# Attention and a gated feed-forward layer with seven-product block matmuls: work shifted by a slot, products reordered, odd tiles paired

## The chip, the core and the metric

The kernel runs on one core of one Trainium2 chip. Five engines work side by side there: TensorE (PE, matmuls; its weight loads are listed as PEld), VectorE (DVE), ScalarE (ACT), GpSimd (POOL, which here issues the loads) and SyncE (SP, which here issues transposes and stores). The metric is the device time of one execution in microseconds (us); lower is better. A profile is one execution recorded instruction by instruction, and its span runs from the first instruction to the last.

## What is computed

```python
# q, k, v: 8 batches, 12 heads, 448 tokens, 64 dims, float32
scores = q @ k.T / sqrt(64) - log(448)
attn   = 1 / (1 + exp(-scores))              # a sigmoid, no row sums
x      = (attn @ v), heads side by side      # 3584 tokens x 768
gate   = max(x @ w_gate, 0)                  # 768 x 1536
val    = x @ w_val                           # 768 x 1536
out    = (gate * val) @ w_out                # 1536 x 768, float32
```

## The kernel before, in words

The matmuls take 16-bit operands and add up in PSUM, which has 8 banks; a ring named `free` hands them out, and `later` (line 84) puts the ones just taken into an order for their next use. The order of all instructions on each engine is the order in which the code below emits them.

**Attention.** A batch is 3 groups of 4 heads. Queries and keys are transposed in 7 chunks of 64 tokens, on PE for batches 0 and 1 and for later ones by DMA: `dma_transposes` (211) makes two DVE copies into `rel` and has SP issue one transposing DMA. `qk_unit` (292) makes the scores of one chunk in two banks, and ACT takes the sigmoid of each into a tile PT. A batch has 21 such units. `pv_group` (300) multiplies a group's 7 tiles with v, and DVE copies the two results to `xT` (184), the transposed input of the feed-forward layer.

**Feed-forward.** Batches 0 and 1 (token group 0) make gate and val by plain matmuls: `gv` (304), one unit for each of 12 blocks of 128 columns. ACT takes the relu and DVE multiplies into `hT` (327). The other token groups, of two batches each, treat gate and val as one 2 x 2 block product, in seven block products instead of eight (a Strassen-Winograd scheme): `gv_pair` (498) does two column blocks at once, 42 matmuls of 448 columns. It needs sums of weight blocks (`unit_sums`, and once for all `gate_sums`, 469) and of input blocks (`batch_sums_t1` and `batch_sums`, 488 and 492), all on DVE. The down projection, `hT` times `wo`, is done for a pair of token tiles of 128 in the same way: `down_pair` (423), 42 matmuls of 384 columns in seven products of six. It needs `weight_sums` (395) once, and four sums for each pair (`token_sums`, 406). With the blocks of a pair's tokens A11, A12, A21, A22 the sums are S1 = A21 + A22, S2 = S1 - A11, S4 = A12 - S2, and S3 = A11 - A21, which overwrites A21 in `hT`. The products are called P1 = A11 B11, P2 = A12 B21, P3 = S4 B22, P4 = A22 T4, P5 = S1 T1, P6 = S2 T2 and P7 = S3 T3. Before the change they are issued in the order P1 P5 P6 P2 P7 P3 P4. Three banks hold them: b takes P1, P6, P7 and P4, c takes P5 and P3, and a takes P2. Between the products ACT and DVE move partial sums to SBUF, and the next product into b or c waits for the copy before it.

A token group has 896 tokens: 7 tiles, three pairs and tile 6, which goes alone through `down` (341): 24 plain matmuls.

**Slots.** The loop from line 684 cuts each batch's 21 units into 5 or 6 slots m. A slot emits 3 to 5 units, perhaps a `pv_group` among them, and then its feed-forward work: a few `gv` (`ffn_mix`, with hooks placed after a count of them), or, from batch 2's last slot on, one item of the queue `work` (`next_work`, 667). An item is "w" (a `gv_pair`), "t" (the single tile) or "y" (a `down_pair`). Small jobs of the slot (transposes for the next batch, batch sums, loads) are emitted inside the item: in a pair behind the copy of P1, by the call `beside()`. `prepare` (659) makes the sums that the next item needs; a pair calls it as `then()` before P4. A group's items are pushed in slot 0 of the following even batch, and what is left after batch 7 runs alone:

```python
    def push_group(g):
        tail = [("t", g, 6)] + [("y", g, p) for p in range(3)]
        if g == 0:
            tail.insert(0, tail.pop(1))
        work.extend([("w", g, f) for f in range(0, NFC, 2) if g > 0] + tail)
```

`hold` (637) is a tiny POOL copy that waits for a transposed tile, so that loads issued behind it start later; `late_loads` (644) places one before v of batch 2 and `wo` (`load_o`, 162). In batch 1 to 3 the loads of the next batch's k, q and v stand behind these on POOL.

Of the kernel before, what the change touches and what calls it, by code (L numbers as in the profile page):

```python
# [17 lines left out]
def kernel(  # L18
# [143 lines left out]
    def load_o():  # L162
        for m0, m1 in ((0, 512), (512, DM)):
            nc.gpsimd.dma_start(
                wo[:, :, m0:m1], moe_w_out[:, m0:m1].rearrange("(c p) m -> p c m", p=P)
            )
# [96 lines left out]
    class FirstSlot:  # L263
# [6 lines left out]
        def unit(self, u):  # L270
# [8 lines left out]
            i = (self.number * 4 + u) % 12  # L279
            PT = early.tile([P, 2, 512], FP16, tag=f"PT{i}", name="PT")  # L280
# [22 lines left out]

    def gv(b, q0, qn, f, act_relu):
# [19 lines left out]
        if g not in hT_tiles:  # L324
            hT_tiles[g] = hTp.tile([P, NFC, 2 * S], FP16, tag="hT", name="hT")
        o = (b % 2) * S + q0
        nc.vector.tensor_tensor(  # L327
            out=hT_tiles[g][:, f, o : o + qn],
            in0=gate_sb[:, 0:qn],
            in1=ps[1][:, 0:qn],  # L330
            op=AOP.mult,
        )
# [8 lines left out]
    def down(g, t):  # L341
        ysb = ysbp.tile([P, DM], FP32, tag="ysb", name="ysb")
        for nm, m0, m1 in (("ya", 0, 512), ("yb", 512, DM)):
            ps = bank(nm)
            for f in range(NFC):
                nc.tensor.matmul(  # L346
                    ps[:, 0 : m1 - m0],
                    hT_tiles[g][:, f, t * P : (t + 1) * P],
                    wo[:, f, m0:m1],
                    start=(f == 0),  # L350
                    stop=(f == NFC - 1),
                )
            nc.vector.tensor_scalar(
                out=ysb[:, m0:m1], in0=ps[:, 0 : m1 - m0], scalar1=OUT_SCALE, scalar2=None, op0=AOP.mult
            )
        store(g, t, ysb, 0, DM, (nc.sync, nc.sync))

# [7 lines left out]
    late = {}  # L365
    sums = {}

    def open_late():
        first_sbuf.close()
        pool = ctx.enter_context(tc.tile_pool(name="late", bufs=1))  # L370
        late["T"] = pool.tile([P, 4, HF, HM], FP16, tag="T", name="T")
        late["X"] = pool.tile([P, 3, HD, S], FP16, tag="X", name="X")
        late["sums"] = ctx.enter_context(tc.tile_pool(name="sums", bufs=2))
# [20 lines left out]

    def weight_sums(i):
        T = [late["T"][:, j] for j in range(4)]
        B11, B21 = wo[:, 0:HF, 0:HM], wo[:, HF:NFC, 0:HM]
        B12, B22 = wo[:, 0:HF, HM:DM], wo[:, HF:NFC, HM:DM]
        sub(T[i], *((B12, B11), (B22, T[0]), (B22, B12), (B21, T[1]))[i])

    def token_blocks(g, p):
        h = hT_tiles[g]
        t1, t2 = (slice(t * P, (t + 1) * P) for t in (2 * p, 2 * p + 1))
        return h[:, 0:HF, t1], h[:, HF:NFC, t1], h[:, 0:HF, t2], h[:, HF:NFC, t2]

    def token_sums(g, p):
# [3 lines left out]
        sub(S2, S1, A11)  # L410
        sub(S4, A12, S2)
        sub(A21, A11, A21)
        sums[("y", g, p)] = S1, S2, S4
# [9 lines left out]
    def down_pair(g, p, beside, then, last, first_copy):  # L423
        A11, A12, S3, A22 = token_blocks(g, p)
        S1, S2, S4 = sums.pop(("y", g, p))
        T1, T2, T3, T4 = (late["T"][:, i] for i in range(4))
        B11, B21, B22 = wo[:, 0:HF, 0:HM], wo[:, HF:NFC, 0:HM], wo[:, HF:NFC, HM:DM]
        y1, y2 = (ysbp.tile([P, DM], FP32, tag="ysb", name="ysb") for _ in range(2))
        lo, hi = slice(0, HM), slice(HM, DM)
        b, c, a = bank("u"), bank("y12"), bank("y11")  # L430
        later((7, 6, 5))
# [10 lines left out]
        first_copy(y1[:, lo], b)  # L442
        beside()
        product(c, S1, T1)
        scaled_act(y2[:, hi], c)
        product(b, S2, T2, False)
        scaled_act(y1[:, hi], b)
        product(a, A12, B21)
        plus(y1[:, lo], a)
        product(b, S3, T3, False)  # L450
        plus(y2[:, hi], b)
        product(c, S4, B22, False)
        plus(y1[:, hi], c)
        if last:
            store(g, 2 * p, y1, 0, DM, (nc.sync, nc.scalar))
        else:
            store(g, 2 * p, y1, 0, DM, (nc.sync, nc.sync))
# [3 lines left out]
        if last:  # L461
            store(g, 2 * p + 1, y2, HM, DM, (nc.sync, nc.sync))
            store(g, 2 * p + 1, y2, 0, HM, (nc.sync, nc.scalar))
        else:
            store(g, 2 * p + 1, y2, 0, DM, (nc.sync, nc.sync))
# [7 lines left out]
    def unit_sums(g, f):  # L473
        S1, S2, S4 = sums_tile(2 * P)
        fs = slice(f * P, (f + 2) * P)
# [5 lines left out]
        sums[("w", g, f)] = S1, S2, S4  # L481
# [10 lines left out]
    def batch_sums(g, ks):  # L492
        T1, T2, T4, _, B21, B12, B22 = batch_blocks(g, ks)
        sub(B12, B22, B12)
        sub(T2, B22, T1)
        sub(T4, B21, T2)

    def gv_pair(g, f, beside, first_copy):
# [3 lines left out]
        b, c, a = ([bank(nm) for _ in range(2)] for nm in ("u", "g2", "g1"))  # L502
        later((6, 7, 4, 5, 2, 3))
        gs = [[gsbp.tile([P, S], FP32, tag="gsb", name="gsb") for _ in range(3)] for _ in range(2)]
        if g not in hT_tiles:
            hT_tiles[g] = hTp.tile([P, NFC, 2 * S], FP16, tag="hT", name="hT")
        h = hT_tiles[g]
        sets = []
        for u in range(2):
            us, fs = slice(u * P, (u + 1) * P), slice((f + u) * P, (f + u + 1) * P)  # L510
            S1, S2, S4 = (t[:, :, us] for t in sums[("w", g, f)])
            sets.append((
                wg[:, 0:HD, fs], wg[:, HD:NDC, fs], wv[:, HD:NDC, fs],
                S1, S2, wv[:, 0:HD, fs], S4,
            ))
        del sums[("w", g, f)]

        def product(ps, i, W, first=True):
            for u in range(2):
                products([(ps[u], S, HD, sets[u][i], W, first)])  # L520

        def copy(i, ps, by=nc.scalar.copy):
            for u in range(2):
                by(gs[u][i][:], ps[u][:, 0:S])  # L524

        def plus(i, ps):
            for u in range(2):
# [4 lines left out]
        def gated(u, o, gate_sb, val):  # L532
            nc.vector.scalar_tensor_tensor(
                out=h[:, f + u, o : o + S], in0=gate_sb, scalar=0.0, in1=val, op0=AOP.max, op1=AOP.mult
            )

        product(b, 0, B11)
        copy(0, b, first_copy)
        product(c, 3, T1)
        copy(2, c)  # L540
        product(b, 4, T2, False)
        copy(1, b)
        beside()
        product(a, 1, B21)
        plus(0, a)
# [5 lines left out]
        for u in range(2):  # L551
            gated(u, 0, gs[u][0][:], b[u][:, 0:S])
        for u in range(2):
            gated(u, S, gs[u][1][:], gs[u][2][:])
# [89 lines left out]
    def late_loads():  # L644
# [3 lines left out]
        load_o()  # L648
# [3 lines left out]

    def push_group(g):
        tail = [("t", g, 6)] + [("y", g, p) for p in range(3)]
        if g == 0:
            tail.insert(0, tail.pop(1))
        work.extend([("w", g, f) for f in range(0, NFC, 2) if g > 0] + tail)
# [9 lines left out]
    def next_work(jobs=(), alone=False):  # L667
        kind, g, i = work.popleft()

        def beside():  # L670
            for job in jobs:
                job()

        if kind == "y":
            down_pair(g, i, beside, prepare, not work, scaled_act if alone else scaled)
        elif kind == "w":
            gv_pair(g, i, lambda: (prepare(), beside()), nc.scalar.copy if alone else nc.vector.tensor_copy)
        else:
            beside()
            prepare()  # L680
            down(g, i)

    ffn_mix(1, [(1, lambda: both(1, 0))])
    for b in range(1, B):
# [16 lines left out]
        elif b == 2:  # L701
            mix = (2, 2, 1, 1, 1, 2)
# [92 lines left out]
```

## Time and profile before

| | us |
|---|---|
| median of three runs (lowest, highest) | 401.42 (400.29, 402.0) |
| the profiled execution, its own time | 400.93 |
| span of that execution | 399.2 |
| pairs of group 0 start, PE | 93.48, 123.14, 132.26 |
| single tiles start, PE | 115.21, 200.07, 291.71, 369.30 |
| last matmul's start group, PE | 392.70 |

The profiled execution stands 0.5 us below the median, and the 1.7 us between its time and its span lie outside the recorded instructions. The mean granted TensorE clock was 0.999. An engine's busy share is a mean over the whole span; what a stage waits for is seen in the list of waits and in the timeline, where each row is a run of like instructions on one engine with its start, its duration, and in brackets the idle time before it with what ended that.

### The profile page before, as it was taken

How to read it: one execution, taken by the hardware profiler on the slowest of the kernel's cores; microseconds unless marked ns; L12 is line 12 of the kernel's file. 1: busy time of each engine (PE TensorE's matmuls, PEld its weight loads, DVE VectorE, ACT ScalarE, POOL GpSimd, SP SyncE). 2: the span in 40 equal slices, each digit the busy share in tenths (PEclk: the TensorE clock that was granted, in tenths of full speed). 3: DMA queues.
4: the chain of work that ended last, by engine and by line, in shares of the span. 5: the costliest groups of instructions: out<-in, count | busy, mean ns of one | idle time of the engine just before them, and what ended most of it. 6: DMA issues, size and time to landing. Idle time of an engine off the chain costs nothing.

```text
span 399.2 us, 8737 instructions
## 1 busy us (share of the span) xinstructions
PE 388.9 (97%) x3488; PEld 217.9 (55%) x3488; DVE 279.9 (70%) x539; ACT 223.0 (56%) x475; POOL 49.4 (12%) x73
## 2 busy tenths in 40 slices
PE   8999999999998999999999999999999999999994
PEld 3678786545455554554555555455455555555562
DVE  2454344367358889999758889999766779887661
ACT  5946778783885565655665455565566234533131
POOL 8643301600030300003000300000000000000000
PEclk9999999999999999999999999999999999999999
DMA  9999994999897894224945695223012320000144
GB/s 149 199 199 204 205 141 94 177 203 187 178 161 152 165 204 76 46 48 51 178 85 133 130 218 89 48 24 61 12 40 80 80 79 2 0 2 0 39 115 124
DMA packets 68793, 43.69 MB, mean 109 GB/s; under 512 B 35856, under 2 KB 65296, under 8 KB 68752
## 3 DMA queue, kind: packets, MB, share of 16 engines
q0 software_dynamic: 30736, 23.33, 39.1%
q1 hardware_dynamic: 37584, 19.24, 23.0%
q8 instruction: 27, 0.44, 0.5%
q10 hardware_dynamic: 432, 0.56, 0.4%
q14 instruction: 14, 0.11, 0.1%
HBM read 47.19 MB, written 11.01 MB: 146 GB/s over the span
## 4 chain that ended last, share of the span: by engine, by line
PE 73%; DMA 14%; issue 6%; POOL 3%; DVE 2%; ACT 1%; ACTq 0%; POOLq 0%; DVEq 0%
PE u L385 32%; PE g L385 15%; PE y L385 9%; DMA v<-in_v_dram 6%; PE qk_ps L232 5%; PE pv_ps L250 5%; DMA wo<-in_moe_w_out_dram 4%; DMA k<-in_k_dram 4%; PE ya L346 3%; PE v_ps L309 1%; PE yb L346 1%; PE g_ps L309 1%; POOL q L110 1%; POOL k L110 1%; DVE wv L376 1%
## 5 line engine op out<-in xcount | busy, mean ns | idle before, releaser
L187 ACT ACTIVATE PT<-qk_ps 128x448 f16<-128x448 f32 (+3 forms) x318 | 150.6, 594 | 71.2 <-PE qk_ps L232 71.1
L385 PEld LDWEIGHTS <-S 128*128 128x128 f16 x540 | 52.8, 98 | 44.4 <-issue 0.8
L528 DVE TENSOR_TENSOR gsb<-g,gsb 128x448 f32<-128x448 f32 x72 | 43.0, 625 | 14.5 <-PE g L385 13.8
L232 PE MATMUL qk_ps<-qkT 64*64 64x448 f16 (+2 forms) x756 | 50.0, 336 | 0.9 <-DVE qkT L206 0.5
L421 ACT ACTIVATE ysb<-u 128x384 f32<-128x384 f32 x27 | 13.4, 498 | 56.3 <-PE u L385 56.3
L327 DVE TENSOR_TENSOR hT<-gate_sb,v_ps 128x256 f16<-128x256 f32 (+2 forms) x36 | 16.2, 465 | 33.5 <-ACT gate_sb L318 22.4
L385 PEld LDWEIGHTS <-hT 128*128 128x128 f16 x288 | 27.7, 98 | 21.0 <-issue 3.2
L524 ACT COPY gsb<-u 128x448 f32<-128x448 f32 x48 | 25.8, 566 | 23.9 <-PE u L385 22.9
L250 PE MATMUL pv_ps<-PT,v 64*64 64x448 f16 (+2 forms) x756 | 37.4, 329 | 0.4 <-issue 0.4
L184 DVE TENSOR_SCALAR xT<-pv_ps 128x448 f16<-128x448 f32 (+2 forms) x53 | 27.9, 567 | 13.4 <-PE pv_ps L250 12.1
L232 PEld LDWEIGHTS <-qkT 64*64 64x64 f16 x756 | 20.3, 105 | 24.9 <-issue 16.3
L309 PE MATMUL v_ps<-xT,wv 128*128 128x256 f16 (+2 forms) x216 | 33.3, 291 | 0.4 <-DVE hT L327 0.2
L309 PE MATMUL g_ps<-xT,wg 128*128 128x256 f16 (+2 forms) x216 | 33.5, 292 | 0.1
L385 PEld LDWEIGHTS <-wv 128*128 128x128 f16 x216 | 21.1, 98 | 19.8
L385 PEld LDWEIGHTS <-wg 128*128 128x128 f16 x216 | 20.3, 98 | 20.6 <-issue 3.0
L250 PEld LDWEIGHTS <-v 64*64 64x64 f16 x756 | 21.8, 107 | 11.8 <-issue 1.4
L385 PE MATMUL u<-T,hT 128*128 128x384 f16 x144 | 27.3, 326 | 0.0
L437 DVE SCALAR_TENSOR_TENSOR ysb<-y,ysb 128x384 f32<-128x384 f32 x24 | 13.4, 557 | 18.8 <-PE y L385 11.3
L110 POOL DMA_DIRECT2D k<-in_k_dram x14 | 10.9, 779 | 112.3 <-DVE rel L215 105.8
L309 PEld LDWEIGHTS <-wg 128*128 128x128 f16 x216 | 18.5, 98 | 11.5 <-issue 5.0
L309 PEld LDWEIGHTS <-wv 128*128 128x128 f16 x216 | 20.1, 98 | 8.2 <-DMA wv<-in_moe_w_val_dram 0.5
L385 PE MATMUL u<-xT,wg 128*128 128x448 f16 x108 | 23.5, 353 | 0.1
(67 smaller groups left out, 531.3 us busy)
## 6 DMA issues: line engine op xcount, KB each, us to landing
out_dram<-ysb SPq DMA_DIRECT2D x53, 192.0 KB, 2.9
k<-in_k_dram POOLq DMA_DIRECT2D x5, 672.0 KB, 11.8
q<-in_q_dram POOLq DMA_DIRECT2D x5, 672.0 KB, 14.9
v<-in_v_dram POOLq DMA_DIRECT2D x8, 336.0 KB, 15.6
v<-in_v_dram POOLq DMA_DIRECT2D x16, 168.0 KB, 15.3
k<-in_k_dram POOLq DMA_DIRECT2D x8, 224.0 KB, 10.4
wo<-in_moe_w_out_dram POOLq DMA_DIRECT2D x1, 1536.0 KB, 13.2
q<-in_q_dram POOLq DMA_DIRECT2D x6, 224.0 KB, 11.3
```

The costliest lines, as they stand in the source:

```text
L110: nc.gpsimd.dma_start(t16[:, xs, cs], rows_of(src, b)[:, xs, cs])
L184: nc.vector.tensor_scalar(out=xT, in0=src, scalar1=XSCALE, scalar2=None, op0=AOP.mult)
L187: nc.scalar.activation(PT_ap, ps_ap, AF.Sigmoid, bias=sig_bias, scale=qk_scale)
L232: nc.tensor.matmul(out_of(hh)[o : o + 64, :], qkT[rows, c, cols], qkT[rows, NCH + c0 : NCH + c1, cols], start=True, stop=True, tile_positi ...
L250: nc.tensor.matmul(ps[hh][64 * r : 64 * r + 64, 0:qn], v16[rows, 2 * g + hh, c * D : (c + 1) * D], pieces[c][rows, hh, :], start=(c == 0), ...
L309: nc.tensor.matmul(ps[-1][:, 0:qn], wt[:, dc, f * P : (f + 1) * P], xT_tiles[b][:, dc, q0 : q0 + qn], start=(dc == 0), stop=(dc == NDC - 1),)
L327: nc.vector.tensor_tensor(out=hT_tiles[g][:, f, o : o + qn], in0=gate_sb[:, 0:qn], in1=ps[1][:, 0:qn], op=AOP.mult,)
L346: nc.tensor.matmul(ps[:, 0 : m1 - m0], hT_tiles[g][:, f, t * P : (t + 1) * P], wo[:, f, m0:m1], start=(f == 0), stop=(f == NFC - 1),)
L385: nc.tensor.matmul(ps[:, 0:n], A[:, k_, :], W[:, k_, :], start=(first and k_ == 0), stop=(k_ == kn - 1), skip_group_check=True,)
L421: nc.scalar.activation(o, ps[:, 0:HM], AF.Copy, scale=OUT_SCALE)
L524: by(gs[u][i][:], ps[u][:, 0:S])
L528: nc.vector.tensor_tensor(out=gs[u][i][:], in0=ps[u][:, 0:S], in1=gs[u][i][:], op=AOP.add)
```

## The change

- The queue: group 0 gives three pairs and no single tile; each odd group gives an additional pair 3, made of tile 6 of the even group before it and its own tile 6. Groups are pushed one slot earlier, in the last slot of their second batch, before that slot takes its item. Batch 2 has no item any more; its slots 4 and 5 swap one `gv`.
- Tile 6 of even groups is written to a tile `aside` of its own. `gated` therefore splits a gate * val over the boundary of column 768 into two instructions; in `gv` relu is now applied a second time within it.
- The products are issued as P1 P2 P6 P5 P7 P3 P4 in pairs and in the gate/val units. `beside()` stands behind P2 in the code.
- `token_sums` makes S1 and S2 only; S4 and S3 are made by `more_token_sums`, in the pair itself, after the jobs of `beside()`. T3 of the down projection overwrites its block in `wo`.
- In the last unit of a group's gate/val the two halves are ordered around `prepare`: even groups do the even batch first and leave the odd one to the next item's `beside()`; odd groups do the odd batch first.
- Batch 3's first two transposes move from batch 2's end to behind the `gv` of its slot 3, with a hold and then the load of `wo`, which is now cut by rows. `gate_sums` and `weight_sums` are spread over batches 2 to 4.
- The attention output of batch 7's last head group is made inside the pair of batch 7's last slot. The PT tiles of the first six slots are laid out otherwise.

```diff
     def load_o():
-        for m0, m1 in ((0, 512), (512, DM)):
+        for i in range(2):
+            cs = slice(i * NFC // 2, (i + 1) * NFC // 2)
             nc.gpsimd.dma_start(
-                wo[:, :, m0:m1], moe_w_out[:, m0:m1].rearrange("(c p) m -> p c m", p=P)
+                wo[:, cs, :], moe_w_out.rearrange("(c p) m -> p c m", p=P)[:, cs, :]
             )
...
+    ASIDE = 6 * P
+
+    def gated(g, f, o, n, gate_sb, val, relu=AOP.max):
...
+        end = o + n
+        cut = max(o, min(end, ASIDE)) if g % 2 == 0 else end
+        for a, z, dst in ((o, cut, hT_tiles[g]), (cut, end, late.get("aside"))):
+            if a < z:
+                d = 0 if dst is hT_tiles[g] else ASIDE
+                nc.vector.scalar_tensor_tensor(
+                    out=dst[:, f, a - d : z - d],
...
         nc.vector.tensor_tensor(out=S1, in0=A21, in1=A22, op=AOP.add)
         sub(S2, S1, A11)
+        sums["y"] = S1, S2, S4
+
+    def more_token_sums(g, p):
+        A11, A12, A21, A22 = token_blocks(g, p)
+        S1, S2, S4 = sums["y"]
         sub(S4, A12, S2)
         sub(A21, A11, A21)
...
         product(b, A11, B11)
         first_copy(y1[:, lo], b)
+        product(a, A12, B21)
         beside()
+        plus(y1[:, lo], a)
+        product(b, S2, T2, False)
+        scaled_act(y1[:, hi], b)
         product(c, S1, T1)
         scaled_act(y2[:, hi], c)
-        product(b, S2, T2, False)
-        scaled_act(y1[:, hi], b)
-        product(a, A12, B21)
-        plus(y1[:, lo], a)
         product(b, S3, T3, False)
         plus(y2[:, hi], b)
+        if last:
+            store(*to2, y2, HM, DM, (nc.sync, nc.sync))
         product(c, S4, B22, False)
         plus(y1[:, hi], c)
...
+        if final == "even":
+            finish((True,))
+            prepare()
+            return lambda: finish((False,))
+        if final == "odd":
+            finish((False,))
+            prepare()
+            finish((True,))
+        else:
+            finish((True, False))
...
     def push_group(g):
-        tail = [("t", g, 6)] + [("y", g, p) for p in range(3)]
-        if g == 0:
-            tail.insert(0, tail.pop(1))
-        work.extend([("w", g, f) for f in range(0, NFC, 2) if g > 0] + tail)
+        if g > 0:
+            work.extend([("w", g, (f, f + 1)) for f in range(0, NFC, 2)])
+        work.extend([("y", g, p) for p in ((3, 0, 1, 2) if g % 2 else (0, 1, 2))])
...
         def beside():
+            while pending:
+                pending.pop()()
             for job in jobs:
                 job()
 
         if kind == "y":
-            down_pair(g, i, beside, prepare, not work, scaled_act if alone else scaled)
...
+            down_pair(
+                g, i, lambda: (beside(), more_token_sums(g, i)), prepare, not work,
+                scaled_act if alone else scaled,
+            )
...
-            mix = (2, 2, 1, 1, 1, 2)
+            mix = (2, 2, 1, 1, 2, 1)
             hooks = {
-                2: [(0, prepare)],
-                4: [(1, lambda: weight_sums(0)), (0, lambda: weight_sums(1))],
-                5: [(1, lambda: weight_sums(2)), (0, lambda: weight_sums(3))],
+                3: [(0, lambda: (dma_transposes(3, 0), dma_transposes(3, 1), hold(3, 1), load_o()))],
+                5: [(0, lambda: (dma_transposes(3, 2), gate_sums(0, 2), gate_sums(2, 4)))],
             }
             open_late()
         elif b == 3:
             mix = (1, 1, 1, 0, 0)
+            hooks = {
+                0: [(0, lambda: (gate_sums(4, 6), gate_sums(6, 8)))],
+                1: [(0, lambda: weight_sums(0))],
+                2: [(0, lambda: (weight_sums(1), prepare()))],
+            }
...
-            if b == 2 and m == count - 1:
-                jobs.append(lambda: (dma_transposes(3, 0), dma_transposes(3, 1)))
+            if b == 3 and m == count - 2:
+                jobs.append(lambda: (weight_sums(2), weight_sums(3)))
+            elif b == 4 and m == 2:
+                jobs.append(lambda: (gate_sums(8, 10), gate_sums(10, 12)))
...
                 if m == count - 1:
+                    push_group(b // 2)
                     jobs.append(lambda: (batch_sums_t1(b // 2), batch_sums(b // 2, (0, 1))))
+                    if b == B - 1:
+                        jobs.append(lambda: (pv_finish(b), batch_sums(b // 2, (1, HD))))
```

## The prediction

> **What bounds the kernel now.** I read the engine totals, then TensorE's waits, then the timelines of TensorE (PE) and VectorE (DVE) through the last stages.
>
> ```profile
> span 399.2 us, 8737 instructions
> ...
> PE 388.9 (97%) x3488; PEld 217.9 (55%) x3488; DVE 279.9 (70%) x539; ACT 223.0 (56%) x475; POOL 49.4 (12%) x73
> ...
> PE 73%; DMA 14%; issue 6%; POOL 3%; DVE 2%; ACT 1%; ACTq 0%; POOLq 0%; DVEq 0%
> ```
> ```profile
> PE u L385 <- DVE xT L184: 1.2, 1, 1.2
> PE u L385 <- DVE ysb L416: 0.6, 1, 0.6
> ...
> PE v_ps L309 <- DVE hT L327: 0.2, 1, 0.2
> ```
>
> PE is busy 97% and holds 73% of the chain that ended last, and from 30 us on it waits only three times that can be seen, all for DVE: 1.16 + 0.57 + 0.20 = 1.93 us. So a microsecond of PE work removed is one of span, and a new wait of PE is one too. The slot of pair 1 of group 0 shows what DVE must do beside one down pair; PE first (columns: start, duration), then DVE:
>
> ```profile
> 123.14 1.14 PE L385 MATMUL u<-wo,hT 128*128 128x384 f16 x6 [1.16 <-DVE xT L184]
> 124.11 1.14 PE L385 MATMUL y<-T,S 128*128 128x384 f16 x6
> 125.09 1.14 PE L385 MATMUL u<-T,S 128*128 128x384 f16 x6
> 126.06 1.14 PE L385 MATMUL y<-wo,hT 128*128 128x384 f16 x6
> 127.04 1.14 PE L385 MATMUL u<-T,hT 128*128 128x384 f16 x6
> ```
> ```profile
> 124.31 0.56 DVE L416 TENSOR_SCALAR ysb<-u 128x384 f32<-128x384 f32 x1 [0.69 <-PE u L385]
> 124.79 0.38 DVE L215 COPY rel<-k 128x896 f16<-128x896 f16 x1
> ...
> 125.99 0.85 DVE L376 TENSOR_TENSOR X<-xT 128x1344 f16<-128x1344 f16 x1
> 126.88 0.39 DVE L376 TENSOR_TENSOR xT<-xT 128x448 f16<-128x448 f16 x1
> 127.19 0.81 DVE L376 TENSOR_TENSOR X<-xT,X 128x448 f16<-128x448 f16 x2
> 127.92 0.55 DVE L437 SCALAR_TENSOR_TENSOR ysb<-y,ysb 128x384 f32<-128x384 f32 x1
> ...
> 130.91 0.56 DVE L376 TENSOR_TENSOR S<-hT,S 128x768 f16<-128x768 f16 x1
> 131.38 0.55 DVE L376 TENSOR_TENSOR hT<-hT 128x768 f16<-128x768 f16 x1
> ```
>
> Read from it: a product (six matmuls) takes 0.975 us; P1's result is copied 1.17 us after the pair's start s (1.18 and 1.19 in the pairs at 205.15 and 214.77); the side jobs (124.79 to 127.92, 3.13 us) lie between that copy and the first addition, and cost PE nothing, since no product before the last waits for anything behind them. The four token sums, the last of which rewrites A21 into S3, are made one slot ahead (the last two lines are those for the next pair).
>
> **What the Trainium skill says.** "TensorE: Matmul & The Clock Gate", section "Architectural detail": VectorE's queue is strictly first in, first out, while TensorE only pulls weight loads ahead. The trace agrees: the addition at 127.92 stands behind jobs it doesn't need, although P2 had ended. Same page, "What's actually happening": the PE clock halves after an idle window of about 3.4 us. Here 1.16 us of waiting left the clock at 1.00; I expect waits under 2.5 us, so no loss of clock. "VectorE: DVE Perf Modes", section on the errata: a fixed cost per instruction. Here 192, 256 and 448 columns (line 327) take 352, 422 and 621 ns, so about 155 ns are fixed. "DMA: Bandwidth & Descriptors", "Issuing engines are not separate DMA queues": all share 16 engines. Here a transpose landed after 12.9 us beside a batch's loads, 4.3 us in the median.
>
> **The change, part by part.**
>
> 1. Tile 6 paired. Four single tiles go (200.07 to 204.07: 4.0 us each; the last 3.9), two pairs of 42 x 0.1625 = 6.83 us come: 15.9 - 13.65 = **-2.3 us** of PE. DVE does about the same.
>
> 2. Sums re-placed. gate_sums leave the slot where they caused the 1.16 us wait, weight_sums the ones of 0.57 and 0.20: **-1.9 us**, the causes being gone.
>
> 3. Product order and split token sums; this is what decides. S4 = A12-S2 and S3 = A11-A21 now are made by more_token_sums, on DVE *behind the jobs of the slot*, while P7, the fifth product, reads S3. P7 could start at s+3.90. DVE: copy at s+1.18, next instruction s+1.66 (0.48 later, as 124.31 to 124.79), jobs J, S4 0.48, A21 0.55, then about 0.2 for signal, weight load and first matmul: s+2.9+J. The wait is J - 1.0 us, where J is above 1.0. Behind the waiting P7 stand P3, P4 and the next slot's scores: nothing else fills PE. By slot:
> - Pair 0 of group 0 (batch 3, slot 3): jobs are two weight sums of 1.28 (start to start, 88.14 to 89.42): 2.56. Besides, DVE comes late: after the last gate*val it does that (two instructions, 0.64), a weight sum 1.28, S1, S2 1.06, so the copy of P1 ends 1.35 us after P1 is there; P6 waits 0.7 for it. P7 then waits 1.7. Sum 2.4.
> - Pair 1 of group 0: J = 3.13 as shown: 2.1.
> - Pair 2 of group 0: two rel copies and the last batch sums, 133.92 to 136.38 = 2.46: 1.45.
> - Pair 1 of group 1: 216.44 to 218.96 = 2.52: 1.5. Pair 2: 225.57 to 228.02 = 2.45: 1.45.
> - Pair 0 of group 2: the odd half of the last unit, four instructions, 1.3: 0.3.
> - Pair 2 of group 2 (batch 7's last slot): T1 and the first batch sums 1.99 (308.08 to 310.08), then batch 7's last PV (1.45 of PE, so P7 may start at s+5.35), its xT copy 0.5, batch sums 1.85; A21 ends at s+7.1: 1.9.
> - Slots with J of 0 to 0.6 (pair 0 of group 1, pair 1 of group 2, all of group 3's 0 to 2): none.
> Sum **+11.1 us**.
>
> 4. Odd groups' last unit. The odd half, S1 and S2 now go before the even half, which frees the u banks. In group 1, the third score unit of the next slot takes those banks. In the trace, that slot's gate*val start at 197.44; two at 0.53, S1 and S2 1.2, two more 1.1 end at 200.85, while the scores were due at 199.59: **+1.3**. Group 3 has no scores there; P1 and P2 read the aside tile, ready long before, and P6 meets S2 just as it ends: **+0.2**.
>
> 5. Aside tile. 24 of the gate*val become two instructions (320 + 128 columns): 24 x 0.155 = 3.7 us more DVE. Half lie in batch 2 and 3, with DVE idle over a second per unit; half in group 2's units, where DVE is busy 9.3 to 9.8 of 10 us, 0.22 to 0.3 more each. P2 earlier gives DVE its 0.7 us waits before the first addition back. I take 0; at worst 1.5.
>
> 6. Loads. Batch 3's k and q no longer queue behind w_out. At 109.50, with free engines, they landed in 6.9 and 9.4 us; issued at 71 they land near 80, before the copies at 83.4. The transposes of groups 0 and 1, then the hold on POOL, let w_out be issued near 91; it needed 16 us (71.95 to 88.04) behind v, so its halves land near 98 and 105. They are needed near 101.5 (weight_sums(0)) and 106.5. Past it on POOL come batch 4's loads, not needed before 120. Taken at 0; if w_out is 3 us late, DVE blocks at its head and PE loses up to 3. The ring of PT tiles for the first slots is reused only after their PV: 0.
>
> 7. Tail. The last pair's y2 upper half is stored before P3 instead of among the last stores on SP, two issues of about 0.5 us: **-0.9** (bounds 0 and -1.1).
>
> Sum: 11.1 + 1.3 + 0.2 - 2.3 - 1.9 - 0.9 = **+7.5 us**. Against the profiled execution's own 400.93 us (span 399.2) this gives 408.4; that execution is 0.5 below the median of the three runs (401.42), so I don't correct for it.
>
> **Rivals.**
> - *The covers hold* (ends faster). The one mechanism: P7 in the seven slots finds S3 ready. Its price point: if DVE's work between P1's end and S3 is less than P6 and P5 cover, 2.9 us less the 1.9 of copy, S4 and S3, nothing is lost. For it: the same jobs cost PE nothing before, and ScalarE or scores may make s later than I think. Against: in five slots J is 2.45 to 3.13, measured, and the order on DVE is fixed. Then 400.9 - 5.1 + 1.5 = 397.3; the change gains as long as the waits of part 3 sum to less than 3.6.
> - *Half covered*: DVE runs ahead in some slots, waits sum to 5: 402.3, the same within what can be told.
> - *A late w_out and a saturated DVE* in group 2 add to the waits: +3 and +1.5: 411 to 413.
> That the change doesn't do what it says I exclude: the four single tiles' 24 matmuls each are gone from the built program's instructions.
>
> **How the numbers follow.** Worked case 73%, its own range 405 to 410.5 (each of eight waits uncertain by 0.3, the tail by 0.9); heavier 12%; half covered 7%; covers hold 8%. Time 408.4. The range 403.5 to 412 leaves out the fast side (about 12%) and the heaviest. A measurement can tell about 0.5% (2 us) from none: faster 0.08, same 0.07, slower 0.85.
>
> **What would show it.** Waits of PE's weight loads or u matmuls for DVE hT (the subtraction of more_token_sums) of 1.3 to 2.5 us in six pair slots, about 11 us in all; a wait of qk_ps for the even gate*val near the first paired tile 6; rows for single tiles gone; the last stores ending sooner after the last matmul. If PE shows less than 4 us of new waits, part 3 is wrong. If a weight sum waits for the w_out DMA, part 6 is.

## The result, and the profile after

| | before | after |
|---|---|---|
| median of four runs each (lowest, highest), us | 401.33 (400.29, 402.0) | 411.72 (411.63, 413.09) |
| span of the profiled execution, us | 399.2 | 409.8 |
| mean granted TensorE clock | 0.999 | 0.994 |

The changed kernel is slower: ratio 1.0269, 95% interval 1.0238 to 1.030, some 10.4 us where 7.5 were forecast. The direction was right, the size was not, and the part of the loss that the forecast lacked has one place. The first lines of the page of the changed kernel, then its list of waits of TensorE (PE; columns: total, times, longest, in us). In these views u is bank b and y stands for the banks a and c:

```profile
span 409.8 us, 8697 instructions
...
PE 389.6 (95%) x3476; PEld 216.2 (53%) x3476; DVE 281.3 (69%) x570; ACT 229.9 (56%) x482; POOL 49.3 (12%) x74
```
```profile
PE u L385 <- DVE hT L376: 6.9, 6, 1.7
PE qk_ps L233 <- DMA qkT<-rel: 4.4, 1, 4.4
...
PE qk_ps L233 <- DVE hT L320: 0.7, 2, 0.5
```

PE is busy as long as before within 0.7 us, in a span 10.6 us longer. The first row is the forecast one: P7, a product into u, waits for the subtraction that makes S3. The last row is the forecast wait of the scores behind group 1's last unit. The second row is in no part of the forecast: scores (qk_ps) wait 4.4 us for a transpose. The timeline of PE around it:

```profile
106.17 0.57 PE L233 MATMUL qk_ps<-qkT 64*64 64x448 f16 x8
111.16 0.96 PE L233 MATMUL qk_ps<-qkT 64*64 64x448 f16 x8 [4.42 <-DMA qkT<-rel]
112.05 2.10 PE L385 MATMUL u<-wo,hT 128*128 128x384 f16 x6
113.95 1.39 PE L385 MATMUL y<-wo,hT 128*128 128x384 f16 x6
115.17 1.14 PE L385 MATMUL u<-T,S 128*128 128x384 f16 x6
...
118.28 1.15 PE L385 MATMUL u<-wo,hT 128*128 128x384 f16 x6 [1.00 <-DVE hT L376]
```

The wait ends at 111.16. The eight score matmuls behind it take 0.96 instead of 0.57 us, P1 2.10 and P2 1.39 instead of 1.14. The windows of two microseconds say why (the figure of 0 to 1 behind the busy times is the granted PE clock):

```profile
108.00:110.00 2.00, 0.00 (x0) 0.00 (x0) 1.16 (x1) 0.51 (x2) 0.00 (x0) 1.00 0.58 74
110.00:112.00 2.00, 0.84 (x8) 0.19 (x8) 1.23 (x3) 0.15 (x1) 0.17 (x1) 0.76 0.01 1
112.00:114.00 2.00, 2.00 (x11) 0.94 (x8) 0.00 (x0) 1.70 (x4) 1.86 (x3) 0.50 0.22 12
114.00:116.00 2.00, 2.00 (x13) 1.15 (x12) 1.80 (x3) 0.00 (x0) 1.75 (x3) 0.89 0.97 131
```

The clock was halved, which cost about 0.4 us on the scores, 0.9 on P1 and 0.25 on P2. The transpose is that of batch 3, group 2. Its issue on SP and that of w_out on POOL, and its landing in the list of DMA issues (the last number is us from issue to landing):

```profile
92.04 1.69 POOL L165 DMA_DIRECT2D wo<-in_moe_w_out_dram  x2 [0.28 <-issue]
```
```profile
95.22 8.30 SPq L220 DMA_TRANSPOSE qkT<-rel  x1
```
```profile
qkT<-rel SPq DMA_TRANSPOSE x1, 15.9
```

It was issued 3.2 us behind w_out and landed after 15.9 us; the two transposes before it, issued at 85 and 87, landed after 4.1 and 4.5 us. The DMA queues, asked in short windows, show how the engines were shared. The first line is 97 to 99 us, the next two 103 to 105, the last 107 to 109; q0 carries the loads, q1 the transposes; columns are packets, MB, and the time that the packets took as a share of the time of 16 engines:

```profile
q0 software_dynamic: 261, 0.40, 112.9%
...
q0 software_dynamic: 224, 0.34, 93.8%
q1 hardware_dynamic: 224, 0.06, 21.7%
...
q1 hardware_dynamic: 956, 0.24, 90.8%
```

At first the transpose moves nothing; then one of its packets goes for each of w_out's, 224 to 224, but w_out's hold 1.5 KB (0.34 MB / 224) and its own 0.26. When w_out is nearly through, by about 107.5, most of the rest go, 956 in 2 us. The Trainium skill says in "DMA: Bandwidth & Descriptors", "Queues, rings and completion order", that an engine goes round its queues packet by packet. The trace agrees in kind, one for one; whether a packet of the profile is a packet of that page no run shows. A transpose here has 1824 packets. Its 15.9 us are 4.0 without any, 7.8 (to 107 us) for 834 of them, one for each of w_out's, 2.0 for the 956, and 2.1 for the last 34 and the signal. The turns explain the second part alone; that nothing moved in the first 4 us is not explained by them.

The P7 waits, in the slot of pair 1 of group 0, PE first, then VectorE (DVE):

```profile
126.95 1.14 PE L385 MATMUL y<-T,S 128*128 128x384 f16 x6
129.76 1.15 PE L385 MATMUL u<-wo,hT 128*128 128x384 f16 x6 [1.67 <-DVE hT L376]
```
```profile
125.20 0.56 DVE L423 TENSOR_SCALAR ysb<-u 128x384 f32<-128x384 f32 x1 [0.81 <-PE u L385]
125.68 0.38 DVE L216 COPY rel<-k 128x896 f16<-128x896 f16 x1
...
128.68 0.55 DVE L376 TENSOR_TENSOR S<-hT,S 128x768 f16<-128x768 f16 x1
129.15 0.55 DVE L376 TENSOR_TENSOR hT<-hT 128x768 f16<-128x768 f16 x1
```

The jobs, J for short, run from 125.68 to 128.68, 3.00 us. S3 ends at 129.70 (129.15 + 0.55), and P7 starts 0.06 us later, where with no wait it would have started at 127.93 (126.95 + 0.975).

Stage by stage, from starts in both traces: late transpose 4.4, half clock 1.6, P7 waits 7.9, P4 of one pair 0.25, group 1's last unit 1.25, group 3's 0.1, tile 6 paired -2.3, waits removed -1.9, tail -0.6. That is 10.7 us, and the spans differ by 10.6.

### The profile page after: what moved, and what is told of

The parts are those of the page before. It is cut to its first block, busy times and chain, and to the rows that moved or that the text cites. A ratio compares the mean times of both kernels' runs of the same rounds, so it can differ in the third digit from the quotient of the medians.

```text
span 409.8 us, 8697 instructions
## 1 busy us (share of the span) xinstructions
PE 389.6 (95%) x3476; PEld 216.2 (53%) x3476; DVE 281.3 (69%) x570; ACT 229.9 (56%) x482; POOL 49.3 (12%) x74
## 5 line engine op out<-in xcount | busy, mean ns | idle before, releaser
L385 PEld LDWEIGHTS <-S 128*128 128x128 f16 x576 | 56.1, 98 | 46.3 <-issue 0.4
L428 ACT ACTIVATE ysb<-u 128x384 f32<-128x384 f32 x32 | 15.7, 490 | 63.3 <-PE u L385 63.1
L385 PEld LDWEIGHTS <-hT 128*128 128x128 f16 x312 | 29.6, 99 | 31.6 <-DVE hT L376 9.7
L531 DVE TENSOR_TENSOR gsb<-g,gsb 128x448 f32<-128x448 f32 x72 | 41.5, 616 | 0.1
L320 DVE SCALAR_TENSOR_TENSOR hT<-gate_sb,v_ps 128x256 f16<-128x256 f32 (+2 forms) x36 | 14.6, 420 | 37.9 <-ACT gate_sb L343 21.0
L185 DVE TENSOR_SCALAR xT<-pv_ps 128x448 f16<-128x448 f32 (+2 forms) x53 | 27.8, 566 | 16.1 <-PE pv_ps L251 15.5
L385 PE MATMUL u<-wo,hT 128*128 128x384 f16 x156 | 30.7, 335 | 7.0 <-DVE hT L376 6.9
L531 DVE TENSOR_TENSOR gsb<-u,gsb 128x448 f32<-128x448 f32 x36 | 21.4, 624 | 15.6 <-PE u L385 15.6
## 6 DMA issues: line engine op xcount, KB each, us to landing
wo<-in_moe_w_out_dram POOLq DMA_DIRECT2D x2, 1152.0 KB, 12.9
k<-in_k_dram POOLq DMA_DIRECT2D x8, 224.0 KB, 10.4
```

Of the source, the lines that this page charges most:

```text
L185: nc.vector.tensor_scalar(out=xT, in0=src, scalar1=XSCALE, scalar2=None, op0=AOP.mult)
L320: nc.vector.scalar_tensor_tensor(out=dst[:, f, a - d : z - d], in0=gate_sb[:, a - o : z - o], scalar=0.0, in1=val[:, a - o : z - o], op0=relu,
L385: nc.tensor.matmul(ps[:, 0:n], A[:, k_, :], W[:, k_, :], start=(first and k_ == 0), stop=(k_ == kn - 1), skip_group_check=True,)
L428: nc.scalar.activation(o, ps[:, 0:HM], AF.Copy, scale=OUT_SCALE)
L531: nc.vector.tensor_tensor(out=gs[u][i][:], in0=ps[u][:, 0:S], in1=gs[u][i][:], op=AOP.add)
```

## The experiments

All times are medians; each ratio is to the kernel before, run on the same chip (401.0 to 401.5 on these), with its 95% interval.

**Is it the place of the sums?** In the changed kernel, S4 and S3 ahead of the jobs:

```diff
-   g, i, lambda: (beside(), more_token_sums(g, i)), prepare, not work,
+   g, i, lambda: (more_token_sums(g, i), beside()), prepare, not work,
```

> The changed kernel with the third and fourth token sums (S4, S3) made ahead of the job additions behind P2, not behind them; nothing else moves. Theory (the P7 waits are the job additions J less about 1.2 us, and only their place in VectorE's queue makes them): all seven P7 waits (7.9 us together) go; in pair 1 of group 0 P4 then waits for T4 behind the same jobs, +0.9: 411.7 - 7.9 + 0.9 = 404.7, between 403.7 and 405.7. Rival (TensorE cannot use the time: the additions or the copies bind at the next product, P3 or P4, of every pair): most of it comes back there and the time stays above 409.

Measured: 406.16 us, ratio 1.0118 (1.009 to 1.0147), 5.6 below the changed kernel. Its timeline of PE in the same slot:

```profile
127.00 1.14 PE L385 MATMUL u<-wo,hT 128*128 128x384 f16 x6
127.97 1.14 PE L385 MATMUL y<-wo,S 128*128 128x384 f16 x6
129.75 1.14 PE L385 MATMUL u<-T,hT 128*128 128x384 f16 x6 [0.65 <-DVE ysb L445]
131.58 0.57 PE L233 MATMUL qk_ps<-qkT 64*64 64x448 f16 x8 [0.69 <-DMA qkT<-rel]
```

P7 (127.00) waits for nothing, here and in every pair. Part of it comes back: P4 waits for an addition that is now behind the jobs (0.80 late here, where it was 0.25 in the changed kernel; 0.24, 0.20 and 0.38 in three other pairs), and the next batch's transposes, issued from a job now 1.0 us later, make the scores wait 0.69. The extra waits are 0.55 + 0.24 + 0.20 + 0.38 + 0.69 = 2.06 us, where 0.9 had been expected, and 7.9 - 2.06 = 5.84 comes near the 5.6. The theory stands; the work that was moved behind has waiters too.

**Or the order of the products?** The kernel before, with its own order, and S4 and S3 behind the jobs:

```diff
         sub(S2, S1, A11)
-        sub(S4, A12, S2)
-        sub(A21, A11, A21)
...
+            g, i, lambda: (beside(), more_token_sums(g, i)), prepare, not work,
```

> The kernel before with one part of the change alone: S4 and S3 are made behind the job additions; its product order and loads stay. In its order S3's product comes sixth too, behind the same jobs. Theory (the place of these sums makes the waits, not the order of the products): the jobs now stand ahead of S3 as in the changed kernel, waits of J less about 1 in the pairs with batch sums or w_out sums, 6 to 8 us in all: 407 to 409. Rival (the order of the products makes the waits; in the old order two more products stand between the jobs and S3, and cover them): 401.3 to 402.5.

Measured: 408.14, ratio 1.0171 (1.0155 to 1.0188): this one move costs 6.9 us. Its waits of PE, and P2 and P7 of pair 1 of group 0:

```profile
PE u L385 <- DVE hT L376: 5.9, 6, 1.8
```
```profile
126.20 1.14 PE L385 MATMUL y<-wo,hT 128*128 128x384 f16 x6
129.13 1.15 PE L385 MATMUL u<-T,hT 128*128 128x384 f16 x6 [1.79 <-DVE hT L376]
```

P7 was due at 126.20 + 0.975 and is 1.96 late; with the old sums' J of 3.13 that is J - 1.17, as in the changed kernel (3.00 and 1.84). S3's product is the fifth in either order (not the sixth, as the expectation has it). P7's waits come from the place of the sums alone.

**Is the slow stretch behind the long wait a matter of clock?** The changed kernel with matmuls put into the wait, whose sums nobody reads:

```diff
+                if b == 3 and (g, c) == (2, 0):
+                    ps = bank("warm_ps")
+                    free.rotate(1)
+                    for _ in range(22):
+                        nc.tensor.matmul(
+                            ps[:, 0:S], wg[:, 0, 0:P], wg[:, 0, P : P + S], start=True, stop=True
+                        )
                 qk_unit(b, g, c)
```

> The changed kernel with 22 matmuls of 448 columns ahead of the first scores of batch 3, group 2, whose sums nobody reads; they run in the time in which TensorE otherwise waits for the late transpose. Theory (the slow products behind that wait are TensorE at a granted clock of 0.50 because it had idled 4.4 us): the clock stays at 1.00 from 107 to 118 us, P1 of pair 0 in group 0 takes 1.14 us instead of 2.10, and the 1.7 us are saved: 410.0, between 409.4 and 410.9. Rival (the clock drops for load, or the products are slow because their weights or additions are late): the products stay slow, 411.7 within 0.5.

Measured: 410.15, ratio 1.0217 (1.0195 to 1.024), 1.6 below the changed kernel. Its timeline, and its window from 112 to 114:

```profile
106.68 4.34 PE L751 MATMUL warm_ps<-wg 128*128 128x448 f16 x22
111.07 0.57 PE L233 MATMUL qk_ps<-qkT 64*64 64x448 f16 x8
111.57 1.15 PE L385 MATMUL u<-wo,hT 128*128 128x384 f16 x6
```
```profile
112.00:114.00 2.00, 2.00 (x14) 1.18 (x13) 1.24 (x2) 1.40 (x4) 2.00 (x4) 1.00 0.79 75
```

The scores start as late as before, but PE is at full speed: the idle time set the clock. That they start as late is chance, and makes the comparison clean. The transpose landed at 109.75 in this profile, and the added matmuls outlasted it by 1.3 us.

**Does w_out hold up the transpose, and where could it go?** Five runs. The first puts w_out back where the kernel before had it:

```diff
         load_v(2)
+        load_o()
...
- 3: [(0, lambda: (dma_transposes(3, 0), dma_transposes(3, 1), hold(3, 1), load_o()))],
+ 3: [(0, lambda: (dma_transposes(3, 0), dma_transposes(3, 1), hold(3, 1)))],
```

> The changed kernel with one thing undone: both halves of w_out are loaded where the kernel before loaded them, behind batch 2's v, instead of between batch 3's transposes. Theory (the transpose of batch 3, group 2 came late because it ran beside w_out's transfers): it lands some 4.3 us after its issue instead of 15.9, the 4.4 us wait of the scores at 107 to 111 us and the half-clock stretch behind it (1.7 us) are gone, the 0.7 us wait of P6 in pair 0 of group 0, which the late transpose had hidden, comes back: 411.7 - 4.4 - 1.7 + 0.7 = 406.3, between 405 and 407.5. Rival (the transpose is late because batch 3's own loads or its place in SyncE's queue delay it, w_out only stands near): it still lands late, 411.7 within 1.

Measured: 416.96, ratio 1.0394 (1.0374 to 1.0413), 5.2 us *above* the changed kernel. The transpose landed after 3.9 us, as the theory wanted, but the list of waits shows a new wait, and DVE's timeline what stands behind it:

```profile
PE g_ps L334 <- DVE xT L185: 8.6, 1, 8.6
```
```profile
95.33 0.39 DVE L216 COPY rel<-q 128x896 f16<-128x896 f16 x1 [2.96 <-DMA q<-in_q_dram]
```

DVE waits 7.0 us to copy batch 3's keys and 3.0 more for its queries, which now come behind w_out; PE waits behind DVE, and its clock is halved for 6.8 us. The changed kernel makes these copies from 84.55, the kernel before from 96.03. So the move of w_out was needed by the earlier transposes; the two belong together.

The second leaves the first half of w_out where the change has it and sends the other half behind the transpose (`load_o` now takes the halves to send, and the hold ahead of batch 4's loads goes):

```diff
- ... hold(3, 1), load_o()))],
- 5: [(0, lambda: (dma_transposes(3, 2), gate_sums(0, 2), gate_sums(2, 4)))],
+ ... hold(3, 1), load_o((0,))))],
+ 5: [(0, lambda: (dma_transposes(3, 2), hold(3, 2), load_o((1,)), gate_sums(0, 2), gate_sums(2, 4)))],
```

> The changed kernel with w_out's second half moved: its first half (rows for P1 and T1) is issued where it was, its second half behind the transposes of batch 3, group 2. The run with all of w_out early came out 5 us slower than the changed kernel, since batch 3's queries then came late; this one leaves those alone. Theory (the transposes are late by sharing the transfers with w_out's 2.3 MB): beside half of it they land in 6 to 8 us, the 4.4 us wait and the half clock behind it (1.7) go, P6's 0.7 us wait comes back, and the second half, some 8 us behind its issue at about 101, costs P2 0 to 2 us: 411.7 - 6.1 + 0.7 + 0.7 = 407, between 406 and 408.5. Rival (w_out's second half takes the place of the wait: P2 and VectorE's T2 stand 4 us or more for it): 410 to 412.

Measured: 415.27, ratio 1.0351 (1.0327 to 1.0374). The transpose took 8.4 us beside half of w_out, and `hold` kept the other half until 104.89. P2 then has the wait, longer than the one removed, and the half clock with it, for 10.2 us:

```profile
115.07 2.10 PE L385 MATMUL y<-wo,hT 128*128 128x384 f16 x6 [6.21 <-DMA wo<-in_moe_w_out_dram]
118.06 2.08 PE L385 MATMUL u<-T,S 128*128 128x384 f16 x6 [0.89 <-DVE ysb L423]
```

That was the rival, and its range of 410 to 412 was still 3 us short. Three more runs move the transpose ahead of batch 2's last `gv` (the FFN unit of the texts below). In the first of them w_out stays:

```diff
- 5: [(0, lambda: (dma_transposes(3, 2), gate_sums(0, 2), gate_sums(2, 4)))],
+ 5: [(1, lambda: dma_transposes(3, 2)), (0, lambda: (gate_sums(0, 2), gate_sums(2, 4)))],
```

> The changed kernel with one thing moved: the transposes of batch 3, group 2 are issued ahead of the last FFN unit of batch 2, not behind it, some 3 us earlier; w_out stays where it is, so both now start together at about 92. Theory (the transposes end about 2 us behind the load they run beside, whenever they start; w_out's 2.3 MB need until about 108): they still take 12 to 16 us and land between 104 and 108, beside the 106.7 at which TensorE asks for them, so most of the 4.4 us wait and the half clock behind it go, and P6's 0.7 us wait for T2 comes back: 411.7 - 6.1 + 0.7 = 406.3, between 405.5 and 408. Rival (only transposes issued behind a load are held up by it): they land in 4 to 6 us, at about 97, the time is the same 406.3, and only the landing tells.

Measured: 408.79, ratio 1.0183 (1.0167 to 1.0199), 2.9 below the changed kernel. Issued at 91.57, 0.3 us ahead of w_out, the transpose landed after 8.5 us, between the two forecasts: in the window of 93 to 95 us it had the engines to itself,

```profile
q1 hardware_dynamic: 1298, 0.33, 99.2%
```

since w_out's data came only after that. The transpose's data had moved by 95.5, which is near the rival. What took the time were its 32 closing packets of 4 bytes, which went from 97.4 to 99.2, beside w_out's. The 4.4 us and the half clock are gone, but not all of the gain is kept: w_out's second half still ends at 108.9, P2 waits 0.50 for it, and P6 waits 1.84 for DVE's copy of P1, since DVE itself had waited for w_out, to make T2. In the changed kernel that was hidden under the wait for the transpose.

The second of them holds w_out back until the transpose has landed (`hold(3, 2), load_o()` behind it, and again no hold ahead of batch 4's loads):

> The same with w_out held back until the transposes of batch 3, group 2 have landed. Theory (a transpose alone lands in 4.3 us; w_out then goes out at about 96.5 and its second half lands 13 us later, at 109.5 to 110): the 4.4 us wait goes, P2 of pair 0 in group 0, due at 108.7, waits 1 to 1.5 us, P6 no longer than that: 411.7 - 6.1 + 1.4 = 407, between 406 and 408.5. Rival (the second half comes later than the pair can bear, since batch 4's loads follow it, as with the two halves apart): P2 waits 4 us or more, 410 to 412.

Measured: 412.02, ratio 1.0262 (1.024 to 1.0284). Alone the transpose took 4.3 us. w_out then went out at 96.21; DVE waited 2.53 us for its first half and 3.14 for its second, PE lost 1.31, 1.43 and 1.84 us in three places from 107 to 114, and the clock fell to 0.50 although no single wait of PE was over 2 us. Neither theory had DVE's wait for the first half.

The third sends w_out's first half directly behind batch 3's v, with no hold:

```diff
- 3: [(0, lambda: (dma_transposes(3, 0), dma_transposes(3, 1), hold(3, 1), load_o()))],
+ 3: [(0, lambda: (dma_transposes(3, 0), dma_transposes(3, 1), hold(3, 1), load_o((1,))))],
...
+                if b == 2:
+                    jobs.append(lambda: load_o((0,)))
```

> The changed kernel with the transposes of batch 3, group 2, ahead of batch 2's last FFN unit, and with w_out's first half issued directly behind batch 3's v, its second half where w_out was. With the transposes alone moved, the time was 408.8; P2 (0.5) and P6 (1.8) of pair 0 in group 0 then stood for w_out's second half and for T2 behind it. Theory (what bounds this stretch is the transfers: w_out ended at 108.9 because it could not start before 92): the first half now fills the pause at 90 to 92, the second half lands 2 us or more earlier, P2's wait goes and P6's falls below 0.5: 408.8 - 0.5 - 1.4 = 406.9, between 406 and 407.8. Rival (the transposes of batch 3, groups 0 and 1 are now slowed beside w_out as group 2's were, and the scores at 93.3 and 101 wait for them): 409 or more.

Measured: 407.74, ratio 1.0164 (1.0148 to 1.018). P2 no longer waits and P6 0.36, as expected; but the rival was there too: group 0's transposes of batch 3 landed after 9.3 us and the scores at 94.17 waited 1.36 for them.

**The order in group 1's last unit.** The even products first:

```diff
-   rest = gv_units(g, i, beside, first_copy, ("even", "odd")[g % 2])
+   rest = gv_units(g, i, beside, first_copy, ("even", "both", "even", "odd")[g])
```

Here "both" finishes the even products, then the odd, then calls `prepare()`.

> The changed kernel with one order changed: in the last w unit of group 1 the products of the gate for the even batch are made before those of the odd one, as in groups 0 and 2, not behind prepare(). Theory (the scores behind that unit wait for the banks which the even products free last, 1.25 us by the starts): 411.7 - 1.25 = 410.4, between 409.9 and 411. Rival (the wait only moves: the odd products or the token sums are then as late for the first pair): 411.7 within 0.4.

Measured: 411.03, ratio 1.0251 (1.0233 to 1.0269), 0.7 below the changed kernel. The two intervals overlap, so this gain is read from the trace more than from the time. The scores' wait is gone, 1.25 us by the starts; 0.40 comes back at P6 of the next pair, which waits for DVE's copy of P1 behind the later token sums. The rest is within the spread of the runs, and the profiled one had 6.8 us at half clock behind the same wait for the transpose, where the changed kernel had 3.4.

**Together.** Sums first, w_out split around the transpose, even first:

> The changed kernel with three edits together: token sums ahead of the jobs, w_out in two halves around the transposes of batch 3, group 2, and even products first in group 1's last unit. Theory (three separate causes, so their gains add): 5.6 (measured for the first alone) + 4.7 (forecast) + 1.25 (forecast) less than 411.7, 400.2, between 398.5 and 402: beside the kernel before nothing that can be told apart, the change's gains (single tile, batch sums, tail) then just paying for what is left of its waits. Rival (they overlap: one TensorE wait taken away is found again at the next late product): 403 to 406.

Measured: 408.49, ratio 1.0188 (1.0169 to 1.0207). The split kept its 6.0 us wait of P2 for w_out, so the forecast of 400.2 failed with it. Beside the split alone (415.27) the other two edits took 6.8 off. The next run puts them beside loads that work better: sums first, even first, and the loads of the run at 407.74.

> The same, with the token sums ahead of the jobs and the even products first in group 1's last unit as well. Theory (three separate causes): 406.9 - 5.6 - 0.7 (both as measured alone) = 400.6, between 399.5 and 402: what the change still gains then pays for the waits that are left, no difference from the kernel before that can be told (401.3). Rival (VectorE stands longer at the head of pair 0 of group 0, as the sums ahead of T4 make T4 late for P4, and takes half of it back): 403 or more.

Measured: 401.27, ratio 1.0003 (0.9994 to 1.0011), as forecast. The main waits of PE that the kernel before did not have:

```profile
PE qk_ps L233 <- DMA qkT<-rel: 1.8, 2, 1.1
...
PE u L385 <- DVE ysb L445: 0.9, 2, 0.6
PE u L385 <- DVE ysb L423: 0.6, 2, 0.4
```

The two edits took 6.5 us off the 407.74; alone they had taken 5.6 and 0.7. Within the noise the causes are separate and the gains add. By the starts, what is left of late products and scores comes to 4.6 us, beside the 4.8 that the change gains (2.3 + 1.9 + 0.6). The last run tries to have the transposes' 1.1 us as well, with all of w_out behind `hold(3, 0)`:

> The changed kernel with token sums ahead of the jobs, even products first in group 1's last unit, the transposes of batch 3, group 2, ahead of batch 2's last FFN unit, and all of w_out behind the landing of group 0's transposes of batch 3 (about 89.5), not group 1's (91.4). With half of w_out sent earlier still, group 0's transposes took 9.1 us and the scores at 93 stood 1.1 us for them. Theory (only transposes that share the transfers with w_out are slowed, and those of groups 1 and 2 have the time): group 0's land in 4.3 us and the 1.1 us go, w_out ends at about 107, so that P2 of pair 0 stands for nothing: 401.3 - 1.1 = 400.2, between 399.5 and 401. Rival (w_out still ends at 108 or later, and P2 and P6 stand 2 us for it and for T2, as they did with the transposes alone moved): 402 to 403.

Measured: 403.02, ratio 1.0039 (1.0023 to 1.0056). Group 0's transposes took 4.1 us and P2 waited for nothing, but:

```profile
92.14 8.96 SPq L220 DMA_TRANSPOSE qkT<-rel  x1
```
```profile
108.26 0.57 PE L233 MATMUL qk_ps<-qkT 64*64 64x448 f16 x8 [1.39 <-DMA qkT<-rel]
...
128.79 0.67 PE L233 MATMUL qk_ps<-qkT 64*64 64x448 f16 x8 [2.25 <-DMA qkT<-rel]
```

w_out now stood 2.1 us ahead of group 2's transpose, and that landed after 16.1 us again. Batch 4's loads wait on POOL for that landing. They went out at 109.2 instead of 103.5, were not through when batch 4's first transpose was issued at 122.15, and that took 6.6 us instead of 5.1. The runs of this kernel spread from 401.87 to 405.37. The four with a mean clock of 1.00 took 401.87 to 402.06; in the profiled one, 403.98, the clock was at 0.50 for 3.4 us behind the wait of 2.25. No version measured is faster than the kernel before.

## Why the prediction was right or wrong

1. *Tile 6 paired, -2.3*: right; the single tiles' rows are gone, and the new pair at 377.53 takes 6.9 us.
2. *Sums re-placed, -1.9*: right; the three waits of the list before are gone.
3. *P7's waits, +11.1*: the mechanism was right, and the runs with the sums moved either way show it. The term was too large: 7.9 was measured. By slot, forecast and measured: pair 0 of group 0 2.4 and 1.15; pair 1 2.1 and 1.84; pair 2 1.45 and 1.04; group 1's pairs 1.5 and 1.23, 1.45 and 1.03; group 2's pair 0 0.3 and 0.03, pair 2 1.9 and 1.57. Three things were mis-sized. P7 starts 0.06 us after S3, not 0.2. With the new order of batch sums J was 3.00, 2.21, 2.40 and 2.20 in the pairs 1 and 2 of groups 0 and 1, not 3.13, 2.46, 2.52 and 2.45; in these four the wait is J - 1.17, not J - 1.0. And in pair 0 of group 0 the late transpose gave DVE time to catch up. In the run at 407.74, where PE does not wait for that transpose, P6 is 0.52 and P7 1.53 late there, 2.05 of the 2.4.
4. *Odd groups' last unit, +1.3 and +0.2*: 1.25 and 0.1 by the starts. Undoing the first gave 0.7, since 0.40 returns at P6.
5. *Aside tile, 0*: right; the list has no wait inside a w unit, and PE is busy 10.00 us of 10 from 250 to 300, though DVE is busy up to 9.75.
6. *Loads, taken at 0*: **the step that failed**, +6.0 us. It asked only whether w_out would be in time for its users, and there it was 4 us off (108.8 instead of 105). It did not ask what w_out does to the transpose issued beside it, though the text itself had quoted one that took 12.9 us beside a batch's loads. The transpose landed after 15.9 us instead of some 4.3, and the scores waited 4.4 us for it. That was long enough to halve the clock, which the forecast had excluded on the ground that no wait would pass 2.5 us: 1.6 more. For that the Trainium skill gives an idle window of about 3.4 us in "TensorE: Matmul & The Clock Gate", "What's actually happening". The trace agrees for this wait: the 3.41 us ahead of the fall at 111.03 held no matmul. But the clock also fell in the run at 403.02, behind a single wait of 2.25 us, so that the forecast's bound of 2.5 would not have been safe either.
7. *Tail, -0.9*: -0.6. From the start of the last product to the end of the span it is 5.9 us instead of 6.5.

The errors of 3 and 6, -3.2 and +6.0, partly cancel, so it is luck that the total was off by no more than 3. The rival of a late w_out and a saturated DVE named a time of 411 to 413, and the time fell there, but not by its mechanism: DVE's wait for w_out, which ended at 108.84, was hidden under PE's wait for the transpose, and in the gate/val units of group 2 PE lost nothing to DVE.

What stays open: why the transpose moves no packet in its first 4 us behind w_out (3.8 to 4.1 us in all nine profiles in which one was issued behind it), and why its issue on SP then lasts 8.3 us instead of 1.5. Which of the two waits for the other, the packets or the issue, no run tells.

## What to carry to other kernels

When a load is moved, look at what runs beside it on the DMA engines, not only at when its own data is needed: the transpose's small packets here got one turn for each of w_out's, 0.06 MB beside 0.34. When work is put behind other work on an engine that, like DVE here, takes it in order, list its users; moving it ahead needs the same list for what it displaces. And before undoing one part of a change, ask which other part made it necessary: here the old place of w_out was worse than the new one.

## What the runs showed of the hardware

- The same transpose landed after 4.3 us alone, 8.5 us issued 0.3 us ahead of w_out, 8.4 us behind half of it, 15.9 us issued 3.2 us behind all of it (14.5 to 16.0 in three more profiles with that order) and 16.1 us issued 2.1 us behind. Behind all of it, its issue held SP for 8.0 to 9.0 us instead of 1.5.
- Issued ahead of w_out, the transpose had moved its data 4.0 us after its issue, and landed 4.5 us later, when its 32 packets of 4 bytes had gone.
- An idle stretch of 4.4 us halved the PE clock at 111.03, and it was back at 114.44, 3.3 us after work had begun again. In each profile the clock fell a whole number of steps of 3.41 us after its first rise (31 steps, 105.81 us, in the changed kernel), and the stretches at half clock between work are one, two or three such steps long. The same wait cost one step in the changed kernel and two in the run with the even products first.
- The clock does not need one long wait. In the step of 3.41 us before it fell, PE was busy 0.00 us in the changed kernel, 1.16 in the run at 403.02 (longest wait 2.25) and 1.49 in the run that held w_out back (a wait of 1.43, and part of one of 1.84). The least busy steps that left it at 1.00 had 1.62 us (the kernel before with its sums moved) and 1.70 (the transpose alone moved).
